# Issuing the sigmoid gate's exponential and the attention's exponential of a chunk as one ScalarE step

## Chip, cores, metric

The kernel runs on one core of a Trainium2 chip. The metric is the device time of one execution in microseconds (us), lower is better.

## The reference

Two branches of the same input x (2048 tokens, width 1024) are mixed by a gate of one number for each token. Cut to what matters:

```python
g = sigmoid((x * gate_w).sum(-1, keepdims=True))
# branch A: 32 heads of width 32, each token attends to 8 earlier positions (distance 0, 2, ... 14)
q, k, v = split(x @ wqkv)
logits = einsum("bhsd,bhswd->bhsw", q, kg) * scale     # masked before the start
a = einsum("bhsw,bhswd->bhsd", softmax(logits), vg) @ wo
# branch B: gated FFN, 1024 -> 3584 -> 1024
b = (gelu_tanh(x @ w_gate) * (x @ w_up)) @ w_down
out = g * a + (1 - g) * b
```

## The kernel before

The sequence is cut into four chunks of 512 tokens, and two chunks make one half of the program. TensorE (PE) does all products, most of them by a scheme that saves products at the price of sums: VectorE (DVE) adds and subtracts weight blocks and activations ("forms"), TensorE multiplies the forms. VectorE also does the whole attention between the products. ScalarE (ACT) does the exponentials, the gelus and copies out of the accumulation banks (PSUM), GpSimd (POOL) and SyncE (SP) issue transfers.

No engine order is written by hand. Several generators ("streams") yield operations. At build time a greedy scheduler takes, again and again, the operation whose modelled start plus the bias of its stream is smallest, and fixes it as the next instruction of its engine. On the chip each engine then works through its fixed list in order. It is a plan made of modelled costs: one operation with another cost or another dependency can change every later choice.

```python
def _start(self, op):                 # modelled start of an operation (cut)
    t = self.clk[op.eng]
    for d in deps:
        t = max(t, d.end + (0.04 if d.eng == op.eng else self.LAT + op.lag))
    return t

def _emit(self, op, t):               # (cut)
    cost = op.cost
    if op.eng == "ACT" and op.table is not None and op.table != self.table:
        self.table = op.table
        cost += 1.29                  # the model knows of table loads only here, after the choice
    ...

def run(self, streams):               # (cut)
    while live:
        best = None
        for s in live:
            ...
            if t is not None and (best is None or t + s[0] < best[0]):
                best = (t + s[0], t, s, op)
        self._emit(op, t)

w.run([(0.0, main()), (0.0, loads()), (0.1, wforms()), (0.1, x_forms()), (0.1, qkv_forms()),
       (0.15, preps()), (0.3, attention()), (0.5, scores())])
```

The gate and the softmax. A chunk's attention is done in two halves, `a` = 0 and 1; the gate is finished with the first of them:

```python
def gate_exp(c):                                                     # L701
    ez, omg, zc = gates[c]
    e = act(0.1, lambda: nc.scalar.activation(out=ez[:], in_=zc[:], func=ACT.Exp), [("zc", c)],
            table="exp", lag=1.0, key=("ez", c))
    yield e

def att_half(c, a, h):
    ...                                                              # logits, maximum, subtraction (L833)
    yield o
    if a == 0:
        yield from gate_exp(c)
    e = act(0.55, lambda: nc.scalar.activation(out=lsb(), in_=lsb(), func=ACT.Exp, scale=scale), [o],
            table="exp", lag=0.6)                                    # L838
    yield e
    if a == 0:
        yield from gate_tail(c)                                      # 1/(1+ez) and its layout, on VectorE
    ...                          # sum, reciprocal, weights (L855), spread (L861), transpose (L870),
                                 # products with v (L879) and their sums
```

The FFN that surrounds it on ScalarE, for each of 28 strips `f` (cut; all matmuls of it have line L927):

```python
ev[f, "m5"] = act(0.48, cp, [o])                # L978: copies bank Dk, "m5"
...                                             # product with T3
gelu of bank A                                  # L996, table "gelu"
...                                             # product 1, copy u2 (L1004)
o = yield from prod(Dk[f], 3, B22, f, False, [ev[f, "m5"]])   # TensorE writes Dk again: needs m5
gelu of the sum                                 # L1012, table "gelu"
```

And the forms of the q, k and v weights that the second half needs:

```python
def qkv_forms():                                # cut
    for f in range(4):
        for kt in range(KH):
            def go(...): V(out=o(), in0=x_(), in1=y_(), op=op)       # L547
            yield dve(t, go, dep, key=("wq", c, which, f, kt), lag=0.5, ...)
```

The first product that TensorE does with them (`prod` of `qkv_pair`, L580) needs all four forms of the first kind, so the fourth L547.

## Time and profile before

| | before |
|---|---|
| time, median of 3 | 741.06 us (740.49 to 744.32) |
| span in the profile | 739.1 us |
| TensorE busy | 723.0 us |
| VectorE busy | 630.6 us |
| ScalarE busy | 321.6 us, 18 of its instructions are table loads of 1.283 us |

The first part of the profile's page (busy time, share of the span and instructions of each engine) of the kernel before:

```profile
PE 723.0 (98%) x3298; PEld 358.0 (48%) x3365; DVE 630.6 (85%) x931; ACT 321.6 (44%) x537; POOL 71.2 (10%) x123
```

TensorE is busy nearly all the time, so only its idle gaps can be won. The waits of TensorE name them (what waited, for whom: us in total, times, longest):

```profile
PE ps L927 <- ACT m L978: 3.1, 2, 1.5
PE ps L580 <- DVE ring L547: 1.6, 1, 1.6
...
PE ps L1068 <- DMA ring<-in_A_wo_dram: 1.0, 2, 0.8
PE ps L1068 <- DMA ring<-oforms: 0.8, 2, 0.6
PE ps L1068 <- DMA ring<-in_B_w_down_dram: 0.2, 1, 0.2
```

The first line is what the change aims at. It is two waits of 1.53 us on L978, the copy m5. The timeline of ScalarE shows why. Its columns are start, duration, instruction, and in brackets idle time before it. This is the second of the two places:

```profile
543.47 1.28 ACT L703 ACT_TABLE_LOAD   x1
544.77 0.21 ACT L703 ACTIVATE ez<-zc 128x16 f32<-128x16 f32 x1
544.89 0.58 ACT L956 COPY ps<-ps 128x512 f32<-128x512 f32 x1
545.49 1.28 ACT L1012 ACT_TABLE_LOAD   x1
546.78 0.63 ACT L1012 ACTIVATE gl<-u 128x512 bf16<-128x512 f32 x1
547.32 0.57 ACT L965 CAST hT<-ps 128x512 bf16<-128x512 f32 x1
547.90 1.28 ACT L838 ACT_TABLE_LOAD   x1
549.20 0.63 ACT L838 ACTIVATE xbuf<-xbuf 128x512 f32<-128x512 f32 x1
549.73 0.57 ACT L978 COPY m<-ps 128x512 f32<-128x512 f32 x1
```

The exponential and the gelu need different table sets, and in the trace each change between them comes with a load of 1.28 us. Here ScalarE loads the table of the exponential for the 0.21 us of the gate, goes back to the gelu's for L1012, and loads the exponential's again for the attention. Three loads stand in one row of work, all ahead of L978 at 549.73. The fourth product of that strip, which writes the bank `Dk` again, needs L978. I call this a double switch; the first place, at 255.8 to 262.6 us, has the same lines.

The second line of the waits, 1.6 us on L547, is of another kind. The timeline of VectorE has the third and the fourth of these forms in the lines at 326.17 and 330.38; the group at 330.38 begins with the fourth:

```profile
326.17 0.36 DVE L547 TENSOR_TENSOR ring<-ring 128x512 bf16<-128x512 bf16 x1
...
330.38 4.44 DVE L547 TENSOR_TENSOR ring<-ring 128x512 bf16<-128x512 bf16 x13
```

The timeline of TensorE at the same place:

```profile
326.96 1.89 PE L580 MATMUL ps<-xr,ring 128*128 128x512 bf16 x8
328.68 0.81 PE L580 MATMUL ps<-tf,ring 128*128 128x512 bf16 x3
331.10 2.75 PE L580 MATMUL ps<-tf,ring 128*128 128x512 bf16 x12 [1.60 <-DVE ring L547]
333.69 5.34 PE L580 MATMUL ps<-xr,ring 128*128 128x512 bf16 x24
```

No idle time stands in VectorE's lines here: it had worked back to back since the last products of the first FFN. So when the fourth L547 lands is set by how much work stands before it in VectorE's order. (The trace before lacks some TensorE records, 3298 of 3365. The one that waited is missing here: the fourth L547 ended at 330.81, and twelve matmuls of 0.216 us are seen from 331.10 to 333.69, so a thirteenth began at about 330.88. The wait was thus about 1.4 us and not 1.6.)

### The profile page before, as it was taken

The numbers are of one execution on the slowest core, as the hardware profiler recorded it, in microseconds if no ns is written. First come the engines' busy times: TensorE is split into PE (matmuls) and PEld (weight loads), VectorE is DVE, ScalarE is ACT, GpSimd is POOL, SyncE is SP. The second block draws the span as 40 slices with busy tenths as digits, with TensorE's granted clock in tenths as the row PEclk, the third lists the DMA queues.
The fourth block names the chain that finished last, engine by engine and source line by source line (L and its number), as shares of the span: only waits on it lengthen the run. The fifth ranks groups of instructions, "written<-read, shape, count | busy, mean of one in ns | idle before, by whom it ended". The sixth has DMA issues, their size and how long they took to land.

```text
span 739.1 us, 9823 instructions
## 1 busy us (share of the span) xinstructions
PE 723.0 (98%) x3298; PEld 358.0 (48%) x3365; DVE 630.6 (85%) x931; ACT 321.6 (44%) x537; POOL 71.2 (10%) x123
## 2 busy tenths in 40 slices
PE   8999999999999999989999999999999999999997
PEld 5666644444444444346565444444444444444443
DVE  2789999999999999999999999999999998954300
ACT  2333455558555661125544212765586557210110
POOL 1234522121212000010000001000000000001000
PEclk9999999999999999999999999999999999999999
DMA  9999955555555459990236999745554644899983
GB/s 306 327 329 357 387 173 167 184 171 177 162 180 180 157 147 316 300 327 28 89 112 192 321 308 324 237 135 164 142 159 130 169 139 161 280 307 332 323 288 120
DMA packets 150435, 162.68 MB, mean 220 GB/s; under 512 B 22896, under 2 KB 110960, under 8 KB 150384
## 3 DMA queue, kind: packets, MB, share of 16 engines
q1 hardware_dynamic: 141552, 134.25, 59.6%
q0 software_dynamic: 8544, 27.27, 10.2%
q8 instruction: 26, 0.43, 0.2%
q10 hardware_dynamic: 288, 0.52, 0.2%
q14 instruction: 25, 0.20, 0.1%
HBM read 129.50 MB, written 28.31 MB: 214 GB/s over the span
## 4 chain that ended last, share of the span: by engine, by line
PE 86%; DVE 7%; DMA 2%; ACT 2%; issue 2%; DVEq 0%; ACTq 0%
PE ps L927 44%; PE ps L1068 21%; PE ps L464 11%; PE ps L580 9%; DVE xbuf L879 1%; DMA ring<-dforms 1%; DVE xbuf L887 1%; DVE xbuf L746 1%; DMA ring<-fforms 1%; DVE hT L1036 1%; DVE xbuf L740 0%; DMA hT<-in_A_x_dram 0%; PE ps L685 0%; PE ps L1163 0%; DVE tf L1036 0%
## 5 line engine op out<-in xcount | busy, mean ns | idle before, releaser
L927 PEld LDWEIGHTS <-ring 128*128 128x128 bf16 x1568 | 153.4, 98 | 188.4 <-issue 3.6
L927 PE MATMUL ps<-xr,ring 128*128 128x512 bf16 x878 | 210.4, 379 | 3.9 <-ACT m L978 3.1
L927 PE MATMUL ps<-tf,ring 128*128 128x512 bf16 x659 | 162.6, 379 | 0.8
L1068 PE MATMUL ps<-ring,hT 128*128 128x512 bf16 x693 | 159.7, 379 | 0.9 <-DMA ring<-in_B_w_down_dram 0.2
L1068 PEld LDWEIGHTS <-hT 128*128 128x128 bf16 x708 | 69.2, 98 | 84.0 <-issue 0.7
L740 DVE TENSOR_TENSOR xbuf<-qo,kT 128x2048 bf16<-128x2048 bf16 x64 | 77.5, 1219 | 2.1 <-ACT kT L486 2.1
L879 DVE TENSOR_TENSOR xbuf<-xbuf,vT 128x2048 bf16<-128x2048 bf16 x64 | 77.4, 1219 | 0.2
L746 DVE TENSOR_TENSOR xbuf<-xbuf 128x2048 bf16<-128x2048 bf16 x56 | 68.2, 1219 | 0.2
L580 PEld LDWEIGHTS <-ring 128*128 128x128 bf16 x336 | 43.8, 131 | 30.3 <-DVE ring L547 1.8
L464 PE MATMUL ps<-xr,ring 128*128 128x512 bf16 x250 | 56.1, 383 | 0.4
L956 ACT COPY ps<-ps 128x512 f32<-128x512 f32 x56 | 32.1, 573 | 52.9 <-PE ps L927 52.9
L1095 POOL DMA_DIRECT2D out_dram<-ost x24 | 13.0, 540 | 431.8 <-ACT ost L1103 338.7
L996 ACT ACTIVATE gl<-ps 128x512 bf16<-128x512 f32 x56 | 33.5, 598 | 46.7 <-PE ps L927 46.1
L1068 PE MATMUL ps<-ring,qo 128*128 128x512 bf16 x189 | 49.2, 379 | 2.1 <-DMA ring<-in_A_wo_dram 1.0
L1103 ACT ACTIVATE ost<-ps,omg 128x512 bf16<-128x512 f32 x16 | 11.0, 686 | 91.8 <-PE ps L1068 91.2
L464 PEld LDWEIGHTS <-ring 128*128 128x128 bf16 x256 | 36.9, 144 | 19.4 <-issue 1.3
L580 PE MATMUL ps<-xr,ring 128*128 128x512 bf16 x188 | 43.2, 379 | 0.3
L1008 DVE TENSOR_TENSOR u<-ps,u 128x512 f32<-128x512 f32 x56 | 38.4, 686 | 5.9 <-PE ps L927 2.7
L433 POOL DMA_DIRECT2D fforms<-ring x56 | 30.4, 543 | 124.6 <-DVE ring L425 109.6
L887 DVE TENSOR_TENSOR xbuf<-xbuf 128x1024 bf16<-128x1024 bf16 x64 | 41.8, 687 | 0.5
L968 DVE TENSOR_TENSOR hT<-hT,gl 128x1024 bf16<-128x1024 bf16 x56 | 38.4, 686 | 3.5 <-ACT hT L965 2.6
L987 DVE TENSOR_TENSOR hT<-ps,m 128x512 bf16<-128x512 f32 x56 | 38.5, 687 | 3.0 <-PE ps L927 2.6
(101 smaller groups left out, 736.2 us busy)
## 6 DMA issues: line engine op xcount, KB each, us to landing
ring<-dforms SPq DMA_DIRECT2D x112, 256.0 KB, 4.7
ring<-in_B_w_down_dram SPq DMA_DIRECT2D x84, 256.0 KB, 4.2
ring<-in_B_w_gate_dram SPq DMA_DIRECT2D x56, 256.0 KB, 5.1
fforms<-ring POOLq DMA_DIRECT2D x56, 256.0 KB, 4.3
ring<-fforms SPq DMA_DIRECT2D x56, 256.0 KB, 3.8
ring<-in_B_w_up_dram SPq DMA_DIRECT2D x42, 256.0 KB, 4.0
ring<-in_A_wqkv_dram SPq DMA_DIRECT2D x40, 256.0 KB, 5.7
ring<-oforms SPq DMA_DIRECT2D x32, 256.0 KB, 5.6
```

Source lines behind the costliest of these rows:

```text
L464: nc.tensor.matmul(banks[bk][:], lhsT=lhsT, rhs=xT(c, kt), start=(kt == 0), stop=(kt == KT - 1))
L580: nc.tensor.matmul(banks[bk][:], lhsT=lhsT, rhs=rhs[:, kt, :], start=(start and kt == 0), stop=(kt == KH - 1), skip_group_check=True)
L740: V(out=w3(box[t]), in0=q_b, in1=k_w, op=ALU.mult)
L746: V(out=w3(box[0]), in0=w3(box[0]), in1=w3(box[t]), op=ALU.add)
L879: return dve(tt(n), taking(("p", t), lambda: V(out=w3(box["p", t]), in0=w3(box["ab"]), in1=v_w, op=ALU.mult)), [("qkv", c, 2, t), abo] + ( ...
L887: V(out=s4(t)[:, t % 2], in0=w3(box["p", t])[:, 0:4], in1=w3(box["p", t])[:, 4:8], op=ALU.add)
L927: nc.tensor.matmul(banks[bk][:], lhsT=wv[:, k, fl * P:(fl + 1) * P], rhs=rhs[:, k, :], start=(start and k == 0), stop=(k == KH - 1), skip_ ...
L968: yield dve(tt(2 * SC), lambda f=f: nc.vector.tensor_tensor(out=hT[:, :, f, :], in0=hT[:, :, f, :], in1=gl[f][:].rearrange("p (j s) -> p j ...
L987: ev[f, "up2"] = dve(tt(SC, True), lambda f=f: nc.vector.tensor_tensor(out=hs(f, 1), in0=v3(banks[Bk[f]][:]), in1=v3(m5[f][:]), op=ALU.add ...
L996: nc.scalar.activation(out=gl[f][:, SC:2 * SC], in_=banks[A[f]][:], func=ACT.Gelu_apprx_tanh)
L1008: e = dve(tt(SC, True), lambda f=f: nc.vector.tensor_tensor(out=u2[f][:], in0=banks[Dk[f]][:], in1=u2[f][:], op=ALU.add), [o, ev[f, "u2"]])
L1068: nc.tensor.matmul(banks[bk][:], lhsT=l, rhs=wv[:, i, :], start=(start and k == 0), stop=(q == last and i == 1), skip_group_check=True)
```

## The change

The gate's exponential and the attention's exponential of the same chunk become one operation. Nothing can be put between them, so both use one load of the table. No arithmetic changes.

```diff
-    def gate_exp(c):
-        ez, omg, zc = gates[c]
-        e = act(0.1, lambda: nc.scalar.activation(out=ez[:], in_=zc[:], func=ACT.Exp), [("zc", c)], table="exp", lag=1.0,
-                key=("ez", c))
-        yield e
-
@@
-        if a == 0:
-            yield from gate_exp(c)
-        e = act(0.55, lambda: nc.scalar.activation(out=lsb(), in_=lsb(), func=ACT.Exp, scale=scale), [o], table="exp",
-                lag=0.6)
+        def exps():
+            if a == 0:
+                nc.scalar.activation(out=gates[c][0][:], in_=gates[c][2][:], func=ACT.Exp)
+            nc.scalar.activation(out=lsb(), in_=lsb(), func=ACT.Exp, scale=scale)
+        e = act(0.65 if a == 0 else 0.55, exps, [o] + ([("zc", c)] if a == 0 else []), table="exp", lag=0.6,
+                key=("ez", c) if a == 0 else None)
```

Two things follow for the scheduler besides the pairing: the gate's exponential now waits for the attention's maximum as well, and the joint operation competes for its place in the order as one. The instruction orders of TensorE, GpSimd and the transfer queue come out the same as before. Those of ScalarE and VectorE differ in many places.

## The prediction

> **What bounds the kernel.** The page's busy table has TensorE (PE) busy for 723.0 of 739.1 us, VectorE (DVE) 85%, ScalarE (ACT) 44%; the granted clock is full throughout. So only PE's idle time can be won, about 16 us, much of it start and tail. The waits of PE name the rest: 3.1 us on ACT's L978 (two waits of 1.53), 1.6 us on DVE's L547, about 2 us on loads. The instruction order of PE, the DMA queue and GpSimd is identical in both kernels; only ACT's and DVE's orders change.
>
> **What the change does.** ACT has 18 table loads of 1.283 us (groups by line); the changed order has 11. No exponential vanishes. Saved: about 9 of 322 us of ACT, an engine with slack. The Trainium skill ("ScalarE: Activation LUTs", What ACT_TABLE_LOAD costs) gives 1283 ns plus a drain of about 1380 ns per switch; the trace confirms the load, but the next instruction follows at once, so I count 1.28 us.
>
> **Where it matters.** The two 1.53 us waits are exactly the double switches: exp table for the gate, gelu table for L1012, exp table again for attention, all before L978, whose copy PE's fourth product of that strip needs (timeline, 255.8-262.6 and 543.5-550.3 us).
> - Second place (about 549 us): after the change one load, the small exponential (0.22) and the attention's (0.63) stand before L978. Worked from trace times, L978 then ends where PE wants it: stall 1.53 -> 0.0 to 0.2. Gain about 1.45 us.
> - First place (about 261 us): both exponentials move behind the last gelu; four loads vanish. Stall 1.53 -> 0 to 0.3, locally a gain of 1.5 us.
>
> **What takes it back.** The chain of waits runs through DVE from 268.5 to 331 us: back-to-back DVE work between the last FFN product and the L547 weight forms on which PE waits at 331.1. In the new DVE order, 6.1 us of attention work of the second chunk (one L855, one L746, two L870, two L879) moves from before the down-projection's forms (L1036) to behind them, and only about 2.8 us (part of the next half's softmax) moves behind the fourth L547. So DVE has about +3.4 us between the two anchors, while it can start L1036 only about 1.8 us earlier (waits on PE and ACT). Estimate: the fourth L547 lands at about 332.4 instead of 330.7; PE reaches that wait 1.5 us earlier, and the wait grows from 1.6 to about 4.8 us. Net at that point: about 1.6 us later than before. With the 1.45 us of the second place the sum is about zero. Everything else (exponentials later in other chunks, no table loads in the last FFN strips) I expect off PE's path.
>
> **Prediction.** 741.2 us, 8 in 10 between 738.5 and 743.5. Chances: faster by over 2%: 0.005; within 2%: 0.985; slower: 0.01.
>
> **What would show it.** Table loads 18 -> 11; ACT busy down by about 9 us; PE's waits on L978 together under 0.5 us; PE's wait on L547 4 to 5.5 us; PE busy unchanged; DVE busy unchanged (630 us), without idle between L1036 and L547 in the first down-projection.
>
> **What would make it wrong.** If DVE reaches L547 no later than before, the result is about 738. If in-order ACT now blocks on DVE (attention exponential or spread copy queued before a PSUM copy that PE needs, around 335 or 425-435 us, or the v copies near 386 us that wait for the previous chunk's attention), a new stall of a few us appears. If the last FFN strip's L1012 at 259 us is late, L978 is late with it and part of the first stall stays.

## More of the kernel before

On one core the executions of one kernel spread by up to about 4 us, so small differences are judged by the ratio of runs that shared a chip, with its 95% interval. Much of this spread goes with the clock that TensorE was granted. Of the 33 executions of the kernel before that ran beside the experiments, 19 had a mean granted clock of 0.999 or more and took 739.62 to 741.36 us (median 739.97); the other 14 had 0.997 or 0.998 and took 741.06 to 743.13 us (median 742.08). The profile of the kernel before shows an execution at full clock.

## The result, and the profile after

The kernel after took 741.92 us (median of 4, 741.64 to 742.30), the kernel before on the same chip 740.77 us (median of 4). The ratio is 1.0009, 95% interval 0.9985 to 1.0032: the same. A ratio is the mean time of one kernel's runs over that of the other's in the same rounds, so it is not quite the ratio of the medians quoted here.

Lines moved: what was L927, L978, L1012, L703 and L838 is L923, L974, L1008, L832 and L833 after; L547, L580 and L685 stayed. The first part of the page of the kernel after:

```profile
PE 727.3 (98%) x3365; PEld 358.2 (48%) x3365; DVE 631.3 (85%) x931; ACT 312.7 (42%) x530; POOL 71.2 (10%) x123
```

The waits of TensorE in the kernel after:

```profile
PE ps L580 <- DVE ring L547: 6.3, 3, 3.9
...
PE ps L1064 <- DMA ring<-in_A_wo_dram: 0.6, 2, 0.4
```

The waits on m5 are gone, and ScalarE lost 8.9 us, which is seven table loads of 1.283 us (18 became 11). The waits on L547 grew from 1.6 to 6.3 us, now in three pieces. TensorE shows more busy time although it does the same matmuls; part of that is records that were missing before, and part is seen below.

The timeline of ScalarE in the kernel after, at the second place:

```profile
554.39 0.58 ACT L961 CAST hT<-ps 128x512 bf16<-128x512 f32 x1
554.98 1.28 ACT L832 ACT_TABLE_LOAD   x1
556.28 0.22 ACT L832 ACTIVATE ez<-zc 128x16 f32<-128x16 f32 x1
556.40 0.61 ACT L833 ACTIVATE xbuf<-xbuf 128x512 f32<-128x512 f32 x1
556.92 0.57 ACT L974 COPY m<-ps 128x512 f32<-128x512 f32 x1
557.50 1.28 ACT L992 ACT_TABLE_LOAD   x1
```

One load, both exponentials, then m5 (L974) at 556.92. The fourth product began at 557.54, 0.05 us after m5 ended, and the waits list nothing for it: ScalarE is just in time. At the first place both exponentials moved behind the last gelu of the FFN, where TensorE did not wait for them.

The timeline of VectorE in the kernel after, around the fourth L547, which is again the first of the group of thirteen:

```profile
327.08 0.43 DVE L547 TENSOR_TENSOR ring<-ring 128x512 bf16<-128x512 bf16 x1
...
331.36 4.44 DVE L547 TENSOR_TENSOR ring<-ring 128x512 bf16<-128x512 bf16 x13
```

And the timeline of TensorE at the same place:

```profile
322.61 1.89 PE L580 MATMUL ps<-xr,ring 128*128 128x512 bf16 x8
324.34 0.38 PE L580 MATMUL ps<-tf,ring 128*128 128x512 bf16 x1
326.07 0.41 PE L580 MATMUL ps<-tf,ring 128*128 128x512 bf16 x1 [1.35 <-DVE ring L547]
327.56 0.41 PE L580 MATMUL ps<-tf,ring 128*128 128x512 bf16 x1 [1.09 <-DVE ring L547]
331.83 4.75 PE L580 MATMUL ps<-tf,ring 128*128 128x512 bf16 x13 [3.86 <-DVE ring L547]
336.42 3.83 PE L580 MATMUL ps<-xr,ring 128*128 128x512 bf16 x17
```

The gate's matmuls (L685) came to an end and the new products (L580) began at 322.61 instead of 326.96: TensorE arrives 4.35 us earlier. Of these, 1.53 us are the wait on m5 and 1.3 us are load waits that this run did not have (0.64 instead of 1.96 us in the down-projection); 0.84 us is the start of the run, where the first FFN product began at 95.21 us before and 94.37 us after. The remaining 0.7 us is how the profile counts a wait: from the modelled end of a matmul, which lies about 0.16 us after the next one could have begun (eight matmuls are shown as 1.89 us, but the next group follows after 1.73). One wait on m5 and three load waits fewer (two instead of five) make four times 0.16 us. But the fourth L547 ended at 331.79 instead of 330.81. All that TensorE had gained, it waited away at this point, and a little more.

Then comes something that the prediction had not thought of. The windows give, for each stretch of time, the busy time of each engine and, in the column after POOL, the granted clock of TensorE. Before:

```profile
328.00:332.00 4.00, 2.40 (x12) 1.26 (x12) 3.96 (x9) 1.73 (x3) 0.00 (x0) 1.00 0.50 186
332.00:335.00 3.00, 3.00 (x16) 1.78 (x15) 2.97 (x11) 2.01 (x4) 0.00 (x0) 1.00 0.00 0
```

And after:

```profile
328.00:332.00 4.00, 0.17 (x1) 0.14 (x2) 3.93 (x8) 0.00 (x0) 0.00 (x0) 0.58 0.00 0
332.00:335.00 3.00, 3.00 (x8) 1.03 (x7) 3.00 (x10) 1.17 (x2) 0.00 (x0) 0.50 0.00 0
```

After the wait of 3.86 us TensorE came back at half clock. Its thirteen matmuls needed 4.59 us until the next group began (331.83 to 336.42), at full clock 2.81 us (13 times 0.216). That is 1.78 us lost.

The sum of the profiles: restart after the fourth L547 +0.95 us (330.88 to 331.83), half clock +1.78, second wait on m5 −1.53: together +1.2. The spans differ by +1.1 us (740.2 and 739.1). The start of the run (0.84 us in favour of after) is inside the first term, so on equal starts the restart was about 1.8 us later.

### The profile page after: what moved, and what is told of

Read it like the earlier page. It is cut to its first block, busy times and chain, and to the rows that moved or that the text cites. A ratio compares the mean times of both kernels' runs of the same rounds, so it can differ in the third digit from the quotient of the medians.

```text
span 740.2 us, 9878 instructions
## 1 busy us (share of the span) xinstructions
PE 727.3 (98%) x3365; PEld 358.2 (48%) x3365; DVE 631.3 (85%) x931; ACT 312.7 (42%) x530; POOL 71.2 (10%) x123
## 4 chain that ended last, share of the span: by engine, by line
PE 95%; DMA 3%; DVE 1%; issue 0%; ACT 0%
PE ps L923 46%; PE ps L1064 28%; PE ps L464 11%; PE ps L580 10%; DMA ring<-in_A_wo_dram 1%; DMA ring<-oforms 1%; DMA ring<-in_A_wqkv_dram 1%; DMA hT<-in_A_x_dram 0%; PE ps L685 0%; PE ps L1159 0%; DVE zt L690 0%; DVE tf L449 0%; DVE tf L446 0%; DVE ring L547 0%; DVE tf L444 0%; DVE xr L448 0%
## 5 line engine op out<-in xcount | busy, mean ns | idle before, releaser
L923 PEld LDWEIGHTS <-ring 128*128 128x128 bf16 x1568 | 153.5, 98 | 185.1 <-issue 0.2
L923 PE MATMUL ps<-xr,ring 128*128 128x512 bf16 x896 | 212.3, 379 | 0.0
L923 PE MATMUL ps<-tf,ring 128*128 128x512 bf16 x672 | 164.0, 379 | 0.0
L580 PEld LDWEIGHTS <-ring 128*128 128x128 bf16 x336 | 44.0, 131 | 37.2 <-DVE ring L547 8.5
L580 PE MATMUL ps<-xr,ring 128*128 128x512 bf16 x192 | 43.4, 379 | 0.0
L983 DVE TENSOR_TENSOR hT<-ps,m 128x512 bf16<-128x512 f32 x56 | 38.5, 687 | 4.1 <-PE ps L923 3.9
```

Of the source, the lines that this page charges most:

```text
L580: nc.tensor.matmul(banks[bk][:], lhsT=lhsT, rhs=rhs[:, kt, :], start=(start and kt == 0), stop=(kt == KH - 1), skip_group_check=True)
L923: nc.tensor.matmul(banks[bk][:], lhsT=wv[:, k, fl * P:(fl + 1) * P], rhs=rhs[:, k, :], start=(start and k == 0), stop=(k == KH - 1), skip_ ...
L983: ev[f, "up2"] = dve(tt(SC, True), lambda f=f: nc.vector.tensor_tensor(out=hs(f, 1), in0=v3(banks[Bk[f]][:]), in1=v3(m5[f][:]), op=ALU.add ...
```

## The experiments

My theory after the result: VectorE's list decides when the fourth L547 lands. So a gain of TensorE ahead of that point (first place) is waited away there, a gain behind it (second place) is kept, and the changed order of VectorE costs a further 1 to 2 us, plus the half clock. The first rival: joining the exponentials costs time at its own places. The second: the table loads themselves matter, and all seven are worth something. The experiments split the change by chunk, repair one suspected cost at a time, and last move the forms to the front. For the kernels that join only some chunks, the condition is one variable:

```diff
+        both = a == 0 and c in SELECTED        # the change: (0, 1, 2, 3); before: ()
-        if a == 0:
+        if a == 0 and not both:
             yield from gate_exp(c)
```

with `both` in the place of `a == 0` in the joint operation. In these kernels L927 and L978 of before are L932 and L983. The runs e1 to e4 shared one chip (before: median 740.85 us of 11), e5 to e8 another (before: 741.36 us of 11), and e9 was run on a third with 11 more of before (740.58 us).

| run | time, median us | ratio to before, 95% interval | table loads | TensorE waits on L547 / m5 in the profile, us |
|---|---|---|---|---|
| after (all chunks) | 741.92 | 1.0009 (0.9985 to 1.0032) | 11 | 6.3 / 0 |
| e1: chunk 0 only | 741.91 | 1.0017 (1.0001 to 1.0034) | 11 | 6.3 / 0 |
| e2: chunks 1, 2, 3 | 739.81 | 0.9982 (0.9966 to 0.9999) | 14 | 4.2 / 0 |
| e3: after, softmax held back | 740.64 | 0.9999 (0.9983 to 1.0015) | 11 | 2.1 / 0 |
| e4: after, TensorE kept busy | 740.66 | 0.9998 (0.9984 to 1.0013) | 11 | (filled) / 0 |
| e5: chunk 3 only | 738.98 | 0.9971 (0.9955 to 0.9988) | 16 | 3.0 / 1.5 |
| e6: chunk 1 only | 741.77 | 1.0009 (0.9993 to 1.0026) | 16 | 4.2 / 1.7 |
| e7: before, forms first | 737.39 | 0.9952 (0.9937 to 0.9967) | 17 | 0 / 2.8 |
| e8: chunks 1, 2, 3, forms first | 735.12 | 0.9922 (0.9907 to 0.9936) | 13 | 0 / 1.2 |
| e9: after, forms first | 745.59 | 1.0061 (1.0045 to 1.0077) | 11 | 0.8 / 0 |

Two notes on reading the table. In the traces of e1, e2, e3, e5 and e6 the first matmul behind the wait on the fourth L547 is missing, as in before (twelve are shown, thirteen in after). The last wait there was therefore 0.2 us (at full clock) to 0.4 us (at half clock) shorter than listed, and I give the restart as the end of the fourth L547. And the granted clock divides the kernels: it was below 0.999 in every execution of after, e1, e6 and e9, in four of five of e2, five of six of e3 and two of six of e5, but in none of e4, e7 and e8. A median of before holds both kinds (four of 11 below 0.999 on the chip of e1 to e4, five of 11 on that of e5 to e8).

### e1: the joint operation for chunk 0 alone

`SELECTED = (0,)`. In the kernel before, chunk 0's two exponentials run at 75.2 and 76.9 us, ahead of the first gelu, and neither needs a table load.

> Only chunk 0's two exponentials are issued as one step; chunks 1 to 3 keep the old two steps. In chunk 0 no table is switched, so nothing is saved there, but the scheduler's VectorE order becomes that of the full change down to L547 (57.5 us of work between the first L1036 and the fourth L547, against 54.1 before). Theory A (the gain on ScalarE is given back by the VectorE order, and the first step of that is chunk 0's): as slow as the full change or slower, 741.5 to 743 us; PE waits on L547 6 to 6.5 us, half clock after it, no wait on the copy m5. Rival B (the order is of no account; time goes with table loads or nothing): 11 loads, as in the full change, and a time equal to before, 740.8.

Measured: 741.91 us, like the whole change. The table loads are 11 and the waits on m5 are gone here too, though no exponential of the chunks 1 to 3 was joined; TensorE waited 6.3 us on L547 and restarted at about 331.7 us at half clock. So an effect like that of the whole change, its gain and its loss, comes out of one operation at 75 us that saves no load itself. It works through the scheduler. On ScalarE a copy of k (L486) stands between the two exponentials before, at 76.42 us; in e1 it follows them, at 75.89 us. On VectorE the first difference stands at 78 us: a sum of the attention's scores, L746, goes ahead of the gate's last steps, L712 to L715. The timeline of VectorE in before has

```profile
78.77 0.17 DVE L712 TENSOR_SCALAR og<-ez 128x16 f32<-128x16 f32 x1
```

right behind an L425, where that of e1 has

```profile
78.11 1.22 DVE L746 TENSOR_TENSOR xbuf<-xbuf 128x2048 bf16<-128x2048 bf16 x1
```

From there on the plan is another one. Up to 265 us the order of VectorE in e1 is that of after; behind that it differs from it in places. The run also says that fewer table loads are no sign of the pairing as such: where the softmaxes fall in the FFN decides how often the tables change.

### e2: the other three chunks

`SELECTED = (1, 2, 3)`, so chunk 0 is as before.

> One step for chunks 1, 2 and 3 only; chunk 0 as before. 14 table loads, both double switches gone, and VectorE keeps nearly its old order (55.3 us between the anchors, L1036 starts with 1.1 us less work before it). Theory A: both waits of 1.53 us on m5 fall below 0.3; PE's wait on L547 becomes about 2.2 us at full clock; 738.0 to 739.5 us, about 2 us below before. Rival B: 740.8, since fewer loads are saved than by the full change. Rival C (the joint step itself blocks ScalarE): 741 to 742.

Measured: 739.81 us, ratio 0.9982 (0.9966 to 0.9999), a few tenths slower than I expected. Both waits on m5 are gone. The restart was at about 329.7 us, 1.1 us earlier than before (0.7 us if both runs are counted from their first FFN product, 94.79 and 95.21 us), so VectorE's order is not spoiled. But TensorE, being earlier, waited 4.2 us there (3.8 with the missing matmul) and not 2.2, and came back partly at half clock: twelve matmuls took 4.27 instead of 2.75 us.

### e5 and e6: one place each

`SELECTED = (3,)` changes the second place (549 us, behind the L547 wait), `SELECTED = (1,)` the first (261 us, ahead of it).

> One step for chunk 3 only, in the second FFN: no QKV weights are formed on VectorE after it. The VectorE order is that of before up to there. Theory A (a saved ScalarE wait is kept where no VectorE-bound stretch follows, and lost where one does): the wait on m5 near 549 us goes, that near 261 us and the 1.6 us on L547 stay; 739.3 us (738.6 to 740.0), 1.45 us below before.

> One step for chunk 1 only: the wait on m5 near 261 us goes, that near 549 us stays. Theory A: PE comes earlier to L547 and waits about 4.2 us there instead of 1.6, and then pays about 1.5 us at half clock; nothing is kept: 741.3 us (740.5 to 742). Rival D (the two places are alike and each saves its 1.5 us): 739.3, as for chunk 3 alone.

Measured: e5 took 738.98 us, ratio 0.9971, and e6 741.77 us, ratio 1.0009. In e5 the wait of 1.53 us at 262 us is still there and that of the second place is gone; in e6 it is the other way round, with 1.53 us left at 552 us. Both take away one wait of the same length. The one behind L547 was kept in full (0.29% of 741 us is 2.1 us, with an interval of 0.9 to 3.3), the one ahead of it was not. The timeline of TensorE in e6 shows where it went:

```profile
330.06 5.33 PE L580 MATMUL ps<-tf,ring 128*128 128x512 bf16 x12 [4.24 <-DVE ring L547]
```

The fourth L547 ended at 329.61 us, 1.2 us earlier than before as read, but only 0.3 us earlier counted from the first FFN products (94.35 and 95.21 us). So of the 1.7 us that TensorE gained at the first place (1.53 and the 0.16 that the profile does not count), about 1.4 were waited away. The thirteen matmuls then took about 5.5 us until the next group at 335.18, 2.7 us more than at full clock, which took the rest and more. Medians alone would not tell these two apart, nor is all of e5's 2.1 us the saved wait: its four executions at 0.999 or more have a median of 738.57 us, the six of before on that chip 739.84, so 1.3 us at equal clock. With this, both runs bear out the first part of the theory. They also refute the rival that each saved load is worth something by itself: e6 has two loads fewer than before and is no faster, and neither are after and e1 with seven fewer. And e5, which is faster, speaks against the first rival, that joining costs time at its own place.

### e3: hold back the softmax that went ahead of the forms

In VectorE's order, steps of the softmax of chunk 1's second half stand ahead of the L547 forms (in the kernel before too, but there other work ahead of them is less). Here the first step of this softmax waits for the fourth of these forms, so that all of it comes later:

```diff
-        o = dve(2.24, taking("z", ...), [("qk", h)], pre=xb_pre(), key=("acct", h))
+        o = dve(2.24, taking("z", ...), [("qk", h)] + ([("wq", 2, 0, 0, KH - 1)] if h == 3 else []), pre=xb_pre(), key=("acct", h))
```

> The full change, and the fourth half's transpose L803 (with the softmax behind it) may only be issued after the fourth L547 of the first QKV weights: 53.5 us of VectorE work between the anchors instead of 57.5. Theory A: PE's wait on L547 falls from 6.3 to about 2.7 us, the clock stays full, 736.4 us (735.5 to 738). Rival B: 741.9, as the full change.

Measured: 740.64 us, ratio 0.9999: missed by 4 us. At the place itself the repair did what it should. The wait on L547 fell to 2.1 us, and TensorE restarted at about 327.2 us at full clock. But the work that was held back now stood ahead of a copy sum of the v products (L641), and TensorE waited there, as its timeline shows:

```profile
386.80 1.89 PE L580 MATMUL ps<-tf,ring 128*128 128x512 bf16 x8 [3.07 <-DVE vT L641]
```

The profiled run was the fastest of the six (738.9 us, granted clock 1.000). The other five took 740.5 to 742.5 us at 0.995 to 0.998, so I take it that they lost a half-clock stretch as well, but no profile shows where. VectorE was busy for 123.2 of the 129 us from 268 to 397 us in this run (windows), so what is taken from one place of its list comes back at the next.

### e4: how much is the half clock?

The whole change, with thirty dummy matmuls just ahead of the first product that needs the forms. They write a bank that this product starts afresh, so results stay right, and TensorE is not idle during the wait:

```diff
+                    if which == 0 and g == 0 and t == 0 and c == 2:
+                        def keep_busy(bk=Dk[t]):
+                            for i in range(30):
+                                nc.tensor.matmul(banks[bk][:], lhsT=ident[:], rhs=B11[:, i % KH, :], start=True, stop=True)
+                        yield Op("PE", 0.0, keep_busy, [fr] if fr else [], tail=0.17)
                     o = prod(Dk[t], which, 0, T1, t, True, [fr])
```

> The full change, with 30 matmuls of no use (into a bank that the next product overwrites) where PE would wait for L547, so that PE is idle for under 1.5 us there. Theory: the fourth L547 lands at the same time, but PE restarts at full clock: about 1.85 us less, 740.1 us (739.6 to 740.6), and the clock record shows no half rate near 330 us. If the half clock after the wait costs nothing: 741.9, or more.

Measured: 740.66 us. Against e1, which has the behaviour of the whole change and ran on the same chip, that is 1.25 us less. The orders of VectorE and ScalarE in its trace are those of after. The granted clock was 0.999 or more in all five runs, against 0.993 to 0.995 in e1. The next group began at 335.30 us instead of 336.42, 1.1 us earlier; the dummies ran on until the restart, so three waiting matmuls (0.65 us) came late, which makes up the 1.78 us. The time was just outside the expected range (739.6 to 740.6). So the half clock is a real term of the loss, of 1 to 2 us, and TensorE waited as long as in after: nothing else moved. With the clock full, what is left of the change is small: the seven executions of before at 0.999 or more on this chip have a median of 740.10 us, 0.56 us less, and the dummies cost 0.65.

### e7 and e8: the forms first

If VectorE's place for L547 is what limits, then it should be moved, whatever the exponentials do. One bias is changed, in the kernel before (e7) and in e2's kernel (e8):

```diff
-    w.run([(0.0, main()), (0.0, loads()), (0.1, wforms()), (0.1, x_forms()), (0.1, qkv_forms()), ...
+    w.run([(0.0, main()), (0.0, loads()), (0.1, wforms()), (0.1, x_forms()), (-1, qkv_forms()), ...
```

> The kernel before, with the QKV weight forms (L547) taken 1 us sooner by the scheduler: 4.6 us less VectorE work stands before the fourth L547. Theory A: PE's wait on L547 (1.6 us) goes, the first double switch stays; the second FFN's exponentials fall in other strips, with three switches close together, so a wait on ScalarE of 0 to 2 us may stand there. 739.3 us (738 to 740.8).

> One step for chunks 1, 2 and 3, and the QKV weight forms taken 1 us sooner: both double switches gone, and 4.6 us less VectorE work before the fourth L547. Theory A: PE's wait on L547 (4.2 us in the run of chunks 1 to 3) falls under 1 us, the clock stays full, VectorE reaches the v copies near 380 us within about 1 us of PE's need: 734.5 to 736.5 us, faster than both kernels. If the VectorE backlog only moves on to the v copies (as with L803 held back, where a wait of 3.1 us appeared): 737 to 738.5.

Measured: e7 took 737.39 us (ratio 0.9952), below the range expected (738 to 740.8); the wait on L547 is gone, the clock is full, and the waits on m5 are still there (2.8 us). e8 took 735.12 us (ratio 0.9922, 0.9907 to 0.9936), as expected, and is the fastest kernel, faster than both kernels by 0.8 to 0.9%. One wait on m5 is left, at 103 us, as its waits of TensorE show:

```profile
PE ps L932 <- ACT m L983: 1.2, 1, 1.2
```

From e7 to e8 the joint operation is worth 2.3 us, where it was worth 1.0 us between before and e2 with the wait on L547 in the way. It is tempting to read this as the gain of the first place, which now passes. The traces do not show that. The timeline of TensorE in e7 has

```profile
335.14 1.89 PE L580 MATMUL ps<-tf,ring 128*128 128x512 bf16 x8
...
558.64 1.67 PE L927 MATMUL ps<-xr,ring 128*128 128x512 bf16 x7 [1.29 <-ACT m L978]
```

and that of e8

```profile
335.13 1.89 PE L580 MATMUL ps<-tf,ring 128*128 128x512 bf16 x8
```

At 335.1 us the two were level: in e8 the wait at 103 us had taken what the first place gave. The 1.4 us by which the profiled spans differ (735.2 and 733.8) arose behind that point, where e7 still waits at 558.64. So e8 is the fastest kernel, but that a gain of the first place passes once VectorE does not hold it up is not shown.

### e9: the whole change with the forms first

e8 joins the chunks 1 to 3. Would joining chunk 0 as well do any harm now?

> The whole change (joint step for all four chunks) with the forms of q, k and v of the second half put first in the greedy choice, as in e7 and e8. If what spoils the change is only that the last form of the second half (L547) lands late, the wait of TensorE there should be gone and the time should fall to about 735 to 737, level with e8 (735.1), because both places where a load of the exponential's table held up the FFN's first multiplications are spared. The rival: chunk 0's joint step spoils something else too, by moving VectorE's work of the gates ahead of other work, so that a new wait appears, like the 3.1 us on the v transposes (L641) in e3; then 737.5 to 739.5, slower than e8 by 2 us or more. [...]

Measured: 745.59 us, ratio 1.0061 (1.0045 to 1.0077). That is slower than every other kernel here, and 10.5 us slower than e8, which differs from it in chunk 0's operation alone (the two ran on different chips; the ratios to before, 1.0061 and 0.9922, say 10.3 us). My expectation missed, and so did the rival's number. The rival's mechanism is what the waits of TensorE in e9 show:

```profile
PE ps L580 <- DVE vT L641: 5.7, 1, 5.7
PE ps L580 <- ACT hT L634: 1.4, 1, 1.4
...
PE ps L580 <- DVE ring L547: 0.8, 2, 0.5
```

The timeline of TensorE around the v products in e8:

```profile
378.29 5.34 PE L580 MATMUL ps<-xr,ring 128*128 128x512 bf16 x23
383.47 1.89 PE L580 MATMUL ps<-tf,ring 128*128 128x512 bf16 x8
385.20 1.89 PE L580 MATMUL ps<-xr,ring 128*128 128x512 bf16 x8
```

The same in e9:

```profile
380.68 5.34 PE L580 MATMUL ps<-xr,ring 128*128 128x512 bf16 x24
391.71 3.46 PE L580 MATMUL ps<-tf,ring 128*128 128x512 bf16 x8 [5.69 <-DVE vT L641]
395.02 1.89 PE L580 MATMUL ps<-xr,ring 128*128 128x512 bf16 x8
```

At 324.4 us the two kernels were level (the first L580 began at 324.41 in e8 and 324.44 in e9). Waits on L547 (0.8 us) and on L634 (1.4 us) made e9 2.4 us late by the group at 380.68. Then TensorE waited 5.7 us for the v sums (L641): in e9's VectorE order four products of the attention with v, sums and folds of them, and one product of the scores stand one after another from 379.83 us on, ahead of L641 at 390.98. In e8 L641 starts at 382.50. The group behind the wait began 8.2 us after e8's, and because its eight matmuls ran at half clock, the next one was 9.8 us late. The spans differ by 9.8 us (743.6 and 733.8). So the account closes: 2.4 us of smaller waits, 5.8 us at L641, 1.6 us half clock.

It says that joining chunk 0 is harmful in all three pairs of kernels that differ in it: before and e1 (+1.1 us by medians, only just clear of the noise), e2 and after (+2.1 us by medians, from two sets of runs), e8 and e9 (+10.5 us).

## Why the prediction was right

The time was right: 741.2 us predicted, 741.92 us measured. The change was foreseen to gain at one place and to lose about as much at another, and that is what happened; e4, which has the change's orders at full clock, lies within 0.6 us of before at full clock. That the number came so close is also in part luck: a term of 1 to 2 us, the half clock, was missing from the sum, and single executions of before differ by more than that. Point by point:

- **Table loads 18 to 11, ScalarE down about 9 us, none of it worth anything by itself.** Right: 11 loads, −8.9 us. e6 shows that loads saved at a place that does not count bring nothing.
- **Waits on m5 under 0.5 us together.** Right: none listed, with m5 ending 0.05 us ahead of the product at the second place. So close a meeting could as well have left a wait of some tenths.
- **"Gain about 1.45 us" at the second place.** Right, and kept: e5 took this place alone and was 2.1 us (0.9 to 3.3) faster than before, 1.3 us at equal clock.
- **The gain of the first place is lost at L547, because VectorE works back to back until then.** Right as far as L547 goes: e6 took this place alone, waited about 1.4 of the 1.7 us away there and lost the rest to the half clock. e7, which moves the forms in the kernel before, gained 0.48% and no longer waits there. That the first place's gain is kept once the forms are moved is not shown, since e8 has a new wait at 103 us.
- **"Net at that point: about 1.6 us later than before."** Held, as far as two single traces say: +0.95 us as read, about +1.8 us when the 0.84 us of the different starts is taken into account.
- **"the wait grows from 1.6 to about 4.8 us".** Off: 6.3 us. The landing of the form was about right; TensorE came earlier than I had thought, by 4.35 us in the traces, where I had counted 1.5. I took the load waits ahead of this point as fixed. They were 2.0 us before and 0.6 us after, and the start of the two runs differed by 0.84 us. A longer wait of this kind costs nothing directly, as the point of restart is VectorE's.
- **"the granted clock is full throughout" was read as a constant.** This term was missing. With a gap of 3.9 us TensorE came back at half clock, 1.78 us by the trace and about 1.25 us by e4. The measured sum is therefore rather +1.2 us than my zero. The Trainium skill, "TensorE: Matmul & The Clock Gate" (Part 1: The HAM clock gate), says that the array falls to half rate after an idle window of about 3.4 us; here it did so in a gap of 3.9 us. I had predicted a gap of 4.8 us and could have looked it up.
- **What I did not see at all is where the new order came from.** The prediction took the changed order as given and told it as a consequence of joining the exponentials at the two places. e1 showed that chunk 0's operation alone, which touches no table load, is enough for the new plan up to 265 us and for its time. The prediction would have been the same, but advice drawn from it would have been wrong: to drop the change is worse than to drop a quarter of it (e2) and move the forms (e8).

What stays open: which of the greedy choices between 78 and 330 us brings the attention ahead of the forms was not traced, and the joint operation with VectorE's order held as it was before was not run. And e3's five unprofiled runs, which were slower than its profiled one, were not explained by a profile.

## What to carry to other kernels

A gain on the busiest engine lasts only as far as the next point where another engine's list decides; before counting it, look for that point, and for how long the busiest engine will then stand still, since a slower clock can come on top: of the seven gaps of 2.6 to 5.7 us in these traces, six ended at half clock. In a kernel whose order is planned by greedy choice, a small local edit is a throw of the whole plan: try it in parts, part by part, and compare the orders of all engines and not just of the one that you edited. Once an edit is found to free one place, put what the next place waits for further ahead; here the two together (e8) gave 0.8%, where each alone gave 0.2 and 0.5%.

## What the Trainium skill lacked or had wrong

- "ScalarE: Activation LUTs" (What ACT_TABLE_LOAD costs) gives about 1283 ns for the load and about 1380 ns for a drain with every switch. The traces show 1.283 us as the mean load in every group of them, and no drain: the load at 554.98 followed the instruction before it within 0.02 us, and the exponential after it began 1.30 us after the load began. Seven loads fewer brought 8.9 us of ScalarE; the page's figures would make it 18.6 us (an estimate, seven times 2.66).
- "TensorE: Matmul & The Clock Gate" (Part 1: The HAM clock gate) was right in kind: the granted clock went to half after gaps of 3.9 us (after and e1) and 5.7 us (e9). Its rule of no idle gaps over about 3 us (Why this matters for your kernels) is not a sharp line here: a gap of 3.07 us ended at full clock in e3 (eight matmuls in 1.89 us, shown above), and a shorter one in e5 at half clock, as the timeline of TensorE shows:

```profile
331.13 4.02 PE L580 MATMUL ps<-tf,ring 128*128 128x512 bf16 x12 [3.01 <-DVE ring L547]
```

  Twelve matmuls took 4.02 us there and 2.75 us in the kernel before. The listed 3.01 us are about 2.6, since the matmul ahead of these twelve is missing and the fourth L547 ended at 330.68 us; the clock was 0.82 in the mean from 329 to 331 us and 0.50 from 331 to 333. The page says (Part 1) that its window runs freely, so gaps of like length can fall on either side; these two runs agree with that. What the runs add is the price of one such gap in a tuned kernel: 1.8 us in after, 1.6 us in e9 and about 2.7 us in e6.
